# A fused SSM convolution and gated GLU on one core: the first loads of x in halves, the other two blocks behind the first weights, transposes one product earlier, ten warming matmuls

## The chip, the cores and the metric

The program runs on one core of one Trainium2 chip. The metric is the device time of the whole program in microseconds. The kernel before takes 239.67 us (median of 3 runs, 239.56 to 239.82).

## What is computed

x has 2048 rows of 640 columns in bf16. The program normalises each row, and adds to x two branches that both read the normalised rows xn: a long convolution over the sequence, gated by xn, and a gated GLU.

```python
x = A_q
xn = (x - mean(x)) / sqrt(var(x) + 1e-5)          # per row of 640
# A: short shift convolution, long FFT convolution, gate by xn
kv = (sum over t of k_pad[:, t:t+S] * shift_k[:, 3-t]) * v
y  = irfft(rfft(kv, 2S) * rfft(ssm_k, 2S))[:S] + kv * ssm_D
A  = xn * y
# B: gated GLU, 640 -> 1728 -> 640
B  = (sigmoid(xn @ w_gate) * (xn @ w_up)) @ w_down
out = x + A + B
```

## The kernel before

The 2048 rows lie as 16 blocks: partition p holds rows 16p to 16p+15, and block b is row b of each partition (128 rows of 640). Four blocks make a group; group 0 is blocks 0 to 3. The GLU works through the four groups one after another. For one group it forms 27 products of w and the transposed xn, each five matmuls of 128x128 weights by 512 columns: per 128 columns of F one gate product (`pg`) and one up product (`pu`), and one mixed product for the 64 columns left over. ScalarE takes the sigmoid of `pg` (line 266), VectorE multiplies it by `pu` into `hT` (line 272), and the down products (`pd`, line 296) follow. Between them lie the steps of the convolution (DFT by matmuls, lines 355 to 456, with round trips through DRAM). The order of all of this is a written string of letters, one per step (`ORDER`, lines 621 to 631), and every engine works through its own instructions in that order.

Ahead of the string stands a prologue, lines 469 to 508, which is where the change lies. It brings the four blocks of group 0 from x to the transposed `xnT`, and does the first two pairs of products while the blocks arrive. Five things matter in it.

- Loads. Two engines issue them: SyncE (SP) and ScalarE (ACT), each with a queue of its own that is worked in order. Lines 469 to 475 issue block 0 on SP, block 1 and then blocks 2 and 3 in one transfer on ACT, then columns 0 to 255 of w_gate on SP and of w_up on ACT, then columns 256 to 511 of both on SP. Each x block is 160 KB (128 rows of 1280 bytes), each piece of weights of 256 columns is 320 KB (640 rows of 512 bytes). The string's first letters (m) go on with the remaining loads on SP. Eight completion semaphores are shared by the loads in turn, so from the ninth load on each waits, before it is issued, for one issued earlier.
- Statistics. For each block VectorE does two `bn_stats` of 320 columns (line 198), one `bn_aggr` (202), one add (210); GpSimd takes the power (214); VectorE normalises (219). The order on VectorE is: statistics of block i, then normalising of block i-1, then aggregation of block i.
- A turn: TensorE transposes a block's five 128x128 pieces into PSUM (line 234) and ScalarE copies them to `xnT` (line 223).
- Quarters: a product of 128 instead of 512 columns, for one block (line 248), five matmuls. The first two gate and up products (`fc` 0 and 1) are made of four quarters each, block by block.
- Warming: matmuls on a zeroed tile whose result nobody reads (line 482), fifteen ahead of the first turn and two behind it.

`pt` and `idle` come from a PSUM pool with two buffers (`psC`), `pg` and `pu` from one with four (`psG`), so a fifth product waits until ScalarE has read the first.

Of the kernel before, what the change touches and what calls it, by code (L numbers as in the profile page):

```python
# [57 lines left out]
def kernel(  # L58
# [14 lines left out]
    nc = tc.nc  # L73
    xr = A_q.flatten_outer_dims().rearrange("(p b) d -> p b d", b=NB)
# [30 lines left out]
    x = res.tile([P, NB, DM], BF16, name="x")  # L105
# [15 lines left out]
    sync = nc.sync  # L121
# [49 lines left out]
    def load_w(eng, lo, hi, u):  # L171
        if u == 0:
            eng.dma_start(w[:, :, lo:hi], wgr[:, :, lo:hi])
            return
        h = min(hi, 13 * P)
        eng.dma_start(w[:, :, UP + lo:UP + h], wur[:, :, lo:h])
        if hi == FF:
            eng.dma_start(w[:, :, FF:UP], wur[:, :, h:FF])
# [51 lines left out]
    def xn_mm(g, i):  # L230
        pool, tag = (psG, "g") if g else (psC, "c")
        xts[i] = pt = pool.tile([P, NC, P], BF16, name="pt", tag=tag)
        for c in range(NC):
            nc.tensor.transpose(pt[:, c, :], xn[:, 4 * g + i, c * P:(c + 1) * P], ident[:])  # L234

    def xn_ev(g, i, copy=act_copy):
        copy(out=xnT[:, i, :, :], in_=xts[i][:, :, :])
# [4 lines left out]
    def quarter(u, fc, i):  # L242

        if i == 0:
            pgs[u, fc] = psG.tile([P, 512], F32, name=("pg", "pu")[u], tag="g")
        o = u * UP + fc * P
        for c in range(NC):
            nc.tensor.matmul(pgs[u, fc][:, i * P:(i + 1) * P], lhsT=w[:, c, o:o + P], rhs=xnT[:, i, c, :],  # L248
                             start=(c == 0), stop=(c == NC - 1))
# [216 lines left out]
        nc.vector.tensor_tensor(xs, xs, chunks[c]["yx", m][:, :, :], ALU.add)  # L466


    sync.dma_start(x[:, 0, :], xr[:, 0, :])
    nc.scalar.dma_start(x[:, 1, :], xr[:, 1, :])  # L470
    nc.scalar.dma_start(x[:, 2:4, :], xr[:, 2:4, :])
    for u in range(2):
        load_w((sync, nc.scalar)[u], 0, 256, u)
    for u in range(2):
        load_w(sync, 256, 512, u)

# [3 lines left out]
    def busy(n):  # L480
        for _ in range(n):
            nc.tensor.matmul(idle[:, :], lhsT=hT[:, 0, 0:P], rhs=hT[:, 0, :], start=True, stop=True)

    def turn(i):
        xn_mm(0, i)
        xn_ev(0, i)


    busy(15)
    for i in range(4):  # L490
        ln_stats(0, i)
        if i:
# [5 lines left out]
    turn(0)  # L498
    busy(2)
    for i in range(4):  # L500
        for fc in range(2):
            for u in range(2):
                quarter(u, fc, i)
            if (i, fc) in ((0, 0), (1, 0), (1, 1)):
                turn(1 + i + fc)
    for fc in range(2):
        gate_ev(0, fc)
        up_ev(0, fc)
# [158 lines left out]
```

## Time and profile before

| | |
|---|---|
| median of 3 runs | 239.67 us (239.56 to 239.82) |
| the profiled execution's own time | 239.41 us |
| its span, first to last instruction | 237.6 us |
| TensorE busy with matmuls | 231.4 us (97%) |
| VectorE busy | 190.3 us (80%) |
| ScalarE busy | 141.2 us (59%) |
| granted TensorE clock, mean | 1.000 |
| DMA | 54.82 MB, 231 GB/s |

The span is counted from the first instruction of the program; what lies around it (239.41 less 237.6) is start and end. A row of the timeline gives the start, the time, engine and line, the operation with what it writes and reads, how many instructions are merged in it, and in brackets the idle time before it with what ended that. A row of stretches gives each engine's busy time in a stretch of the span, the granted clock, the share of the DMA engines and the rate. A list of waits gives who waited for what, in total, how often and at most. The clock in these rows is what the throttle granted; whether a matmul ran at half speed at the very start is read from the spacing of the matmuls instead.

### The profile page before, as it was taken

Reading aid. Unit: us, or ns where it says so; the run is one execution under the profiler, and the core shown is the slowest. Engines: PE = TensorE matmul, PEld = TensorE weight load, DVE = VectorE, ACT = ScalarE, POOL = GpSimd, SP = SyncE. Lnnn points to the kernel's source line nnn. Section 1 sums busy time; section 2 is a strip of 40 time slices with the busy share of each in tenths; the row PEclk is TensorE's granted clock in tenths of the full one; section 3 lists DMA queues with packets and bytes.
Section 4 is the critical chain, followed back from the end, with each engine's and each line's share of the span. In section 5 each row is a group of like instructions: output and inputs, shape, how many; then the busy total and the mean of one; then the engine's idle time right before and its main releaser. Section 6 shows DMA issues by size and latency. Waiting matters only on the chain.

```text
span 237.6 us, 5553 instructions
## 1 busy us (share of the span) xinstructions
PE 231.4 (97%) x2265; PEld 135.1 (57%) x2265; DVE 190.3 (80%) x350; ACT 141.2 (59%) x178; POOL 11.2 (5%) x24
## 2 busy tenths in 40 slices
PE   8799999999999999999999999999999999999994
PEld 2564445878556455667754434577664434456782
DVE  3633889999999999999999999865585695968372
ACT  2342331728559897864888887997558858764000
POOL 4210000020000000002001000000000000000000
PEclk9999999999999999999999999999999999999999
DMA  7999999889998999999444888975939795285674
GB/s 212 292 314 233 259 322 298 183 249 284 253 311 243 253 295 297 284 267 319 148 183 152 234 230 258 227 228 203 241 109 222 186 281 123 89 238 144 196 237 134
DMA packets 88975, 54.82 MB, mean 231 GB/s; under 512 B 47670, under 2 KB 83062, under 8 KB 88694
## 3 DMA queue, kind: packets, MB, share of 16 engines
q1 hardware_dynamic: 88006, 53.66, 80.8%
q10 hardware_dynamic: 944, 0.82, 1.1%
q8 instruction: 17, 0.28, 0.5%
q14 instruction: 8, 0.07, 0.1%
HBM read 36.12 MB, written 18.35 MB: 229 GB/s over the span
## 4 chain that ended last, share of the span: by engine, by line
PE 95%; DMA 3%; ACT 0%; DVE 0%; ACTq 0%; issue 0%
PE pd L296 26%; PE pg L257 23%; PE pu L257 23%; PE psb L456 4%; PE ps L357 4%; PE ps L355 4%; PE ps L388 3%; DMA w<-in_B_w_up_dram 3%; PE psa L417 2%; PE pg L278 2%; PE pt L234 2%; PE pu L248 1%; PE pg L248 1%; ACT xnT L223 0%; DVE x L301 0%; ACT L119 0%
## 5 line engine op out<-in xcount | busy, mean ns | idle before, releaser
L257 PEld LDWEIGHTS <-w 128*128 128x128 bf16 x500 | 46.5, 98 | 54.3 <-issue 5.3
L296 PE MATMUL pd<-wd,hT 128*128 128x320 bf16 x448 | 64.3, 299 | 0.0
L257 PE MATMUL pg<-xnT,w 128*128 128x512 bf16 x250 | 62.2, 379 | 0.0
L257 PE MATMUL pu<-xnT,w 128*128 128x512 bf16 x250 | 62.1, 379 | 0.0
L296 PEld LDWEIGHTS <-hT 128*128 128x128 bf16 x448 | 42.8, 98 | 17.8 <-issue 1.7
L266 ACT ACTIVATE sig<-pg 128x512 bf16<-128x512 f32 x52 | 31.3, 605 | 30.1 <-PE pg L257 28.2
L272 DVE TENSOR_TENSOR hT<-sig,pu 128x512 bf16<-128x512 bf16 x52 | 35.2, 679 | 14.7 <-PE pu L257 9.3
L223 ACT CAST t<-ps 128x1024 bf16<-128x1024 f32 x40 | 39.1, 1023 | 11.4 <-DMA d<-t 6.3
L223 ACT CAST xz<-ps 128x1024 bf16<-128x1024 f32 x40 | 38.6, 1018 | 10.6 <-PE ps L388 10.5
L301 DVE TENSOR_TENSOR x<-pd,x 128x320 bf16<-128x320 f32 x32 | 15.4, 480 | 15.8 <-PE pd L296 15.7
L403 DVE TENSOR_TENSOR xz<-xz 128x2048 bf16<-128x2048 bf16 x20 | 24.4, 1220 | 0.2
L357 PE MATMUL ps<-kvh,S1t 128*128 128x128 bf16 x160 | 21.2, 219 | 0.0
L335 DVE TENSOR_TENSOR acc<-acc,tmp 128x1024 bf16<-128x1024 bf16 x30 | 20.7, 689 | 0.7
L355 PE MATMUL ps<-kvh,S1t 128*128 128x128 bf16 x160 | 21.2, 217 | 0.0
L333 DVE TENSOR_TENSOR tmp<-kx,sc 128x1024 bf16<-128x1024 bf16 x30 | 20.6, 687 | 0.4
L223 ACT CAST ao<-psa 128x1024 bf16<-128x1024 f32 x16 | 15.6, 1014 | 5.6 <-PE psa L417 3.5
L461 DVE TENSOR_TENSOR yx<-psb,xn 128x512 bf16<-128x512 f32 x20 | 13.8, 691 | 3.9 <-PE psb L456 2.9
L355 PEld LDWEIGHTS <-S1t 128*128 128x128 bf16 x160 | 15.5, 97 | 2.3
L357 PEld LDWEIGHTS <-S1t 128*128 128x128 bf16 x160 | 15.3, 96 | 2.3
L223 ACT COPY xnT<-pt 128x640 bf16<-128x640 bf16 x16 | 10.2, 709 | 10.8 <-PE pt L234 10.5
L198 DVE BATCH_NORM_STATS2 st<-x 128x6 f32<-128x320 bf16 x32 | 13.7, 471 | 2.8 <-DMA x<-in_A_q_dram 2.8
L401 DVE STREAM_SHUFFLE xz<-xz 128x512 f32<-128x512 f32 x20 | 14.6, 728 | 0.0
(44 smaller groups left out, 146.1 us busy)
## 6 DMA issues: line engine op xcount, KB each, us to landing
d<-t SPq DMA_DIRECT2D x20, 512.0 KB, 3.7
t<-d SPq DMA_DIRECT2D x20, 512.0 KB, 4.9
bi<-d SPq DMA_DIRECT2D x8, 512.0 KB, 5.5
d<-ao SPq DMA_DIRECT2D x6, 512.0 KB, 4.1
kx<-in_A_k_dram SPq DMA_DIRECT2D x10, 256.0 KB, 5.0
hn<-in_A_ssm_k_dram SPq DMA_DIRECT2D x20, 128.0 KB, 6.0
kvh<-in_A_v_dram SPq DMA_DIRECT2D x10, 256.0 KB, 5.2
x<-in_A_q_dram SPq DMA_DIRECT2D x3, 640.0 KB
```

Source lines behind the costliest of these rows:

```text
L223: nc.scalar.copy(out=out, in_=in_)
L257: nc.tensor.matmul(pg[:, :], lhsT=w[:, c, u * UP + fc * P:u * UP + (fc + 1) * P], rhs=xnT[:, :, c, :], start=(c == 0), stop=(c == NC - 1))
L266: nc.scalar.activation(sig[fc][:, :], pgs[0, fc][:, :], ACT.Sigmoid)
L272: nc.vector.tensor_tensor(hT[:, fc, :], sig[fc][:, :], pgs[1, fc][:, :], ALU.mult)
L296: nc.tensor.matmul(pd[:, :], lhsT=hT[:, fc, bb * P:(bb + 1) * P], rhs=wd[:, fc, 320 * half:320 * half + 320], start=(fc == 0), stop=(fc == ...
L301: nc.vector.tensor_tensor(x[:, 4 * t + bb, es], pds[bb, half][:, :], x[:, 4 * t + bb, es], ALU.add)
L333: nc.vector.tensor_tensor(d["tmp"][:, :, :], kx[:, lo + 3 - m:hi + 3 - m, :], sb(m), ALU.mult)
L335: nc.vector.tensor_tensor(d["acc"][:, :, :], d["acc"][:, :, :], d["tmp"][:, :, :], ALU.add)
L355: nc.tensor.matmul(ps[:, i, 0:P], lhsT=S1[:, b, h, :], rhs=cin[c]["kvh"][:, 0, b, :], start=True, stop=True)
L357: nc.tensor.matmul(ps[:, i, P:2 * P], lhsT=S1[:, b, h, :], rhs=hp[:, b // 2, b % 2, :], start=True, stop=True)
L401: nc.vector.stream_shuffle(z[:, 2, :, :].bitcast(F32), z[:, 1, :, :].bitcast(F32), swap)
L403: nc.vector.tensor_tensor(z[:, 1:3, :, :], z[:, 0:1, :, :].to_broadcast((P, 2, 8, P)), z[:, 1:3, :, :], ALU.mult)
```

## The change

Six things change, all in the prologue. Blocks 0 and 1 of x are loaded in column halves, one half on SP and the other on ACT, block 0 first. The first weights (columns 0 to 255) come next, ahead of blocks 2 and 3. Blocks 2 and 3 follow as one transfer each, block 2 on SP and block 3 on ACT. Then SP goes on as before. There are ten warming matmuls ahead of the first turn instead of fifteen. The turn of block i+1 is issued behind the first quarter of block i; before, turn 1 came behind the first two quarters of block 0, turn 2 behind the first two of block 1, and turn 3 behind the last of block 1. For block 0 the two gate quarters now come ahead of the two up quarters.

```diff
-    sync.dma_start(x[:, 0, :], xr[:, 0, :])
-    nc.scalar.dma_start(x[:, 1, :], xr[:, 1, :])
-    nc.scalar.dma_start(x[:, 2:4, :], xr[:, 2:4, :])
-    for u in range(2):
-        load_w((sync, nc.scalar)[u], 0, 256, u)
+    for b in range(2):
+        for i in range(2):
+            (sync, nc.scalar)[i].dma_start(x[:, b, 320 * i:320 * i + 320], xr[:, b, 320 * i:320 * i + 320])
+    for i in range(2):
+        load_w((sync, nc.scalar)[i], 0, 256, i)
+    for i in range(2):
+        (sync, nc.scalar)[i].dma_start(x[:, 2 + i, :], xr[:, 2 + i, :])
     for u in range(2):
         load_w(sync, 256, 512, u)
...
-    busy(15)
+    busy(10)
...
     turn(0)
     busy(2)
     for i in range(4):
-        for fc in range(2):
-            for u in range(2):
-                quarter(u, fc, i)
-            if (i, fc) in ((0, 0), (1, 0), (1, 1)):
-                turn(1 + i + fc)
+        for k in range(4):
+            fc, u = divmod(k, 2) if i else (k % 2, k // 2)
+            quarter(u, fc, i)
+            if k == 0 and i < 3:
+                turn(i + 1)
```

## The prediction

> **What bounds the kernel now.** I read the page's busy times first, then TensorE's waits, then the timeline of the first 15 us. TensorE's waits, all of them:
>
> ```profile
> PE idle L482 <- DVE hT L117: 1.2, 1, 1.2
> PE pu L248 <- DMA w<-in_B_w_up_dram: 0.6, 1, 0.6
> PE pt L234 <- DVE xn L219: 0.6, 1, 0.6
> PE pg L248 <- ACT xnT L223: 0.6, 2, 0.3
> ```
>
> All four lie in the prologue. The stretch from the first full product to the last matmul has no gap (220.02 us busy of 220.06):
>
> ```profile
> 14.34:234.40 220.06, 220.02 (x2151) 1.00 0.82 231
> ```
>
> So the end is the start of the first full product, 14.34, plus 223.26 us that the change does not touch: 237.6 in all, and 1.81 us around the span give 239.41 in the profiled execution (the median of the runs is 0.26 above it). The question is when line 257 starts. The timeline of the prologue:
>
> ```profile
> 3.97 0.89 DVE L198 BATCH_NORM_STATS2 st<-x 128x6 f32<-128x320 bf16 x2 [2.85 <-DMA x<-in_A_q_dram]
> ...
> 6.71 0.88 DVE L198 BATCH_NORM_STATS2 st<-x 128x6 f32<-128x320 bf16 x2
> ...
> 7.50 0.43 DVE L219 TENSOR_SCALAR xn<-x,mv,rstd 128x640 bf16<-128x640 bf16 x1
> ...
> 8.81 0.45 PE L248 MATMUL pu<-xnT,w 128*128 128x128 bf16 x5 [0.60 <-DMA w<-in_B_w_up_dram]
> ...
> 9.10 0.44 PE L234 MATMUL pt<-ident,xn 128*128 128x128 bf16 x5
> ...
> 10.32 0.44 PE L248 MATMUL pg<-xnT,w 128*128 128x128 bf16 x5 [0.22 <-ACT xnT L223]
> ...
> 10.35 0.45 DVE L219 TENSOR_SCALAR xn<-x,mv,rstd 128x640 bf16<-128x640 bf16 x1 [0.66 <-POOL rstd L214]
> ...
> 14.34 1.24 PE L257 MATMUL pg<-xnT,w 128*128 128x512 bf16 x5
> ```
>
> Block 0 arrives at 3.95. VectorE then works without a gap until 9.7; a block takes it 1.45 us (statistics at 5.21, 6.71, 8.16). TensorE stands from 8.2 to 8.81 for w_up, which ACT issued at 1.65 behind 480 KB of x; the chain of waits names it too (1.65 7.12 DMA w<-in_B_w_up_dram). From 8.81 TensorE is nearly full: fifteen quarters and three turns of 0.28 us each (spacing 0.056 us) are 5.0 of the 5.53 us to 14.34.
>
> How fast the loads move, by stretches of 1 us (last column GB/s):
>
> ```profile
> 2.00:3.00 1.00, 1.00 (x4) 0.44 (x3) 0.00 (x0) 0.65 (x2) 1.00 (x3) 1.00 0.77 212
> 3.00:4.00 1.00, 1.00 (x4) 0.32 (x3) 0.03 (x1) 0.00 (x0) 0.04 (x1) 1.00 1.11 367
> 4.00:5.00 1.00, 1.00 (x6) 0.44 (x5) 0.97 (x3) 0.00 (x0) 0.00 (x0) 1.00 1.05 372
> 5.00:6.00 1.00, 0.97 (x5) 0.24 (x3) 0.96 (x4) 0.00 (x0) 0.56 (x1) 1.00 1.13 303
> ```
>
> The DMA engines are full from 3 us on, so an order of loads decides who comes early; nothing comes early for free.
>
> **The change, part by part.**
>
> *Fewer warming matmuls.* Before, fifteen run from 1.18 to 5.97: by their weight loads seven at a spacing of 0.43 (1.58, 2.01 to 3.72), from 4.08 on seven in 1.39, 0.2 each. The tenth of these ends at 4.9. The first turn waits for xn of block 0 (6.54 before, later than both), so they cost and save nothing on the path. What covers this is the clock staying up (a rival below).
>
> *Loads.* Ahead of the first weights stand 328 kB (x0, x1) in place of 655 kB, so w_gate and w_up of columns 0 to 255 have moved when 983 kB have. By the rates above (0.02 MB before 2 us, then 0.21, 0.37, 0.37) that is 5.0 us, and with the lag from last packet to landing 5.8 to 6.1. The lag is about 0.7: the ACT queue's packets of w_up end near 8.05 and it lands at 8.77. The wait at 8.81 is gone; the first quarter, at 7.5, finds both weights. What is late next is block 2. SP now issues two halves, w_gate, then block 2, its fourth DMA (issues there take 0.39 to 0.53 us, so about 2.1; block 2 left ACT at 1.22 before), and in the rings 983 kB stand ahead of blocks 2 and 3. All 1311 kB have moved at 6.1 by the same rates (1.27 MB by 6.0, then 293 GB/s). To that come 0.15 for the 512 packets of 640 bytes (an estimate: between half of a 1280-byte packet's time, no loss, and the whole, 0.9 us), 0.7 of lag and 0.15 because the engines do not finish together: block 2 lands at 7.1. Bounds: 6.4, if ACT's queue falls behind SP's as it did before, and 7.9, if the small packets cost like whole ones.
>
> *What is queued behind block 2.* VectorE's statistics of block 2 wait for it, and in its order the normalising of block 1 stands behind them, though its rstd is long there. Before, these statistics ran at 6.71; with block 0 landing a little sooner (two queues share its 160 KB; I take 3.7, bounds 3.4 and 4.1) VectorE could begin them at 6.45. They start at 7.1.
>
> *Turns.* From those statistics on, by rows: xn of block 1 ends 1.22 later (6.71 to 7.93), turn 1 begins 0.06 after that, its quarter 1.22 after the turn (9.10 to 10.32: transposes, ScalarE's copy of 0.69, two hand-overs), the next turn one quarter (0.28) later. That is 1.50 per turn in the new order; VectorE's xn comes every 1.43 and is ahead (xn2 2.67, xn3 4.09 after the statistics, turns 2 and 3 at 2.78 and 4.28). TensorE has five groups of 0.28 in each 1.50, so it is not the limit either. Block 3's first quarter comes 1.50+1.50+1.22 = 4.22 after turn 1, and the first full product four quarters later (1.12; ScalarE's first sigmoid frees its buffer just then, as before). The sum from the statistics of block 2: 1.22+0.06+4.22+1.12 = 6.62.
>
> *The sum.* 7.1+6.6 = 13.7 against 14.34: 0.6 us sooner. The later weights do not bind: the order behind 1311 kB is unchanged, columns 512 to 767 of w_gate are issued around 2.8 before and are used four products after 14.34. After 14.34 everything moves up with TensorE, except loads that the DMA rate fixes. The nearest is the first half of k: VectorE's first kv step is at 23.85, its load was issued at 15.28 with 7.6 us to landing (about 22.9), so about 1 us of slack, enough for 0.6. Profiled 239.41 - 0.6 = 238.8; on the median 239.67 - 0.6 = 239.1.
>
> *A rule that speaks against the split.* The Trainium skill's DMA: Bandwidth & Descriptors (Issuing engines are not separate DMA queues) says that DMAs from different engines end up on the same 16 DMA engines and interleave, so that spreading them saves only issue time. By it the halves bring block 0 no sooner than 3.95; the forecast of 239.1 stays, since block 2 binds, but the best case below would end at 238.7 instead of 238.3. The trace agrees so far as the rate stays near 290 to 370 GB/s with one queue or two.
>
> **Rivals.**
>
> 1. *Block 2 early; VectorE is the limit.* w_up was issued with the second w_gate piece (1.65 and 1.64), yet landed at 8.77 against 7.9: between 5 and 6 us ACT's queue moved 108 packets and SP's 496. If ACT again begins its weights late, w_gate has the engines to itself and block 2 lands by 6.4. Then VectorE's own chain counts: block 0 at 3.4 to 3.7, statistics of block 2 at 2.74 later, 6.62 more: 12.8 to 13.1, so 238.1 to 238.5. Against it: both weights are now issued alike. Chance 0.13.
> 2. *Hidden anyway.* Block 2 at 7.4 to 7.9, or a later load that takes the gain back: first product 14.0 to 14.5, 239.3 to 239.9. For it: DMA share 1.0 and more up to 25 us. Chance 0.15.
> 3. *Slower by the clock.* Between the tenth warming matmul (4.9) and turn 1 (8.4) TensorE has only turn 0, two warming matmuls and one quarter, 1.0 us of work in 3.4. If the clock drops, 128-column matmuls take twice 0.056, the five groups of a turn's period 2.7 in place of 1.5, and 2 to 3.4 us at half speed cost 0.8 to 1.4 us: 239.9 to 240.5. It decides against the change once more than 0.6 us is lost. Against it: from 232.7 to 236.1 TensorE was busy 1.66 of 3.4 and in 6 to 9 us 1.51 of 3.0, at full clock. Chance 0.13.
>
> The Trainium skill's TensorE: Matmul & The Clock Gate (What's actually happening) puts the gate on free-running windows of about 3.4 us, one busy to open, one idle to close. By it ten matmuls at 0.43 are 4.3 us, enough to open, and no gap here is a whole window, so 239.1 would stand. The trace opened after 2.9 us; how busy a window must be no run here shows.
>
> 4. *Block 3 late.* It is ACT's fourth DMA and waits, by the eight semaphores, for a half of block 0 (about 3.8, plus 0.4 to issue), behind SP's later weights. From its landing to the first product are 2.64 (8.16 to 10.80) + 0.06 + 1.22 + 1.12 = 5.04, so it decides from 9.3 on; at 9.8 the time is 240.2. Against it: only w_up stands ahead in its own queue. Chance 0.07.
>
> **Numbers.** The forecast (block 2 between 6.5 and 7.4, 238.4 to 239.4) has 0.52. A measurement tells about 0.2%, 0.48 us, from no change, so below 239.19 is faster and above 240.15 slower. Faster: 0.33 of the forecast's 0.52 (block 2 before 7.2) and rival 1, 0.46. Slower: 0.09 of rival 3, 0.05 of rival 4 and 0.03 of rival 2, whose later loads may cost more than the gain, 0.17. The same: the rest, 0.37. The range leaves out the lower part of rival 1 (0.05) and most of what is slower (0.14): 238.3 to 240.2.
>
> **What would show it.** No wait of `pu` for w_up; VectorE's second long wait ended by DMA of x ahead of the statistics of block 2, at about 7.1; turns 1.5 apart; line 257 first at 13.7; matmuls without a gap after it. Wrong if spacing in the quarters is 0.11 (clock), if block 3 is what VectorE waits for, or if new waits on DMA appear after 14 us.

## The result, and the profile after

The changed kernel takes 243.57 us (median of 4 runs, 242.03 to 244.18) beside 239.75 us for the kernel before (4 runs, 239.56 to 241.14): a ratio of 1.0141 [1.0107, 1.0176], so 1.4% slower. The forecast was 239.1, with a range from 238.3 to 240.2. The profiled execution took 243.84 us with a span of 242.1, against 239.41 and 237.6 before: 4.5 us more span.

TensorE's waits in the profile after (who waits for what; total, times, longest):

```profile
PE pt L234 <- DVE xn L219: 1.8, 2, 1.3
PE pg L248 <- DMA w<-in_B_w_gate_dram: 1.4, 1, 1.4
PE idle L484 <- DVE hT L117: 1.2, 1, 1.2
PE psa L417 <- ACT t L223: 0.8, 2, 0.5
```

The wait for w_up is gone, as forecast. In its place stand a wait for w_gate, one for a normalised block, and one far from the edit: `psa` (line 417) near 127 us. The timeline after shows how the prologue ran (start, time, engine and line, operation, and in brackets the idle time before it with what ended that):

```profile
3.00 0.89 DVE L198 BATCH_NORM_STATS2 st<-x 128x6 f32<-128x320 bf16 x2 [1.88 <-DMA x<-in_A_q_dram]
...
5.57 0.45 PE L234 MATMUL pt<-ident,xn 128*128 128x128 bf16 x5 [0.49 <-DVE xn L219]
...
7.82 0.71 PE L248 MATMUL pg<-xnT,w 128*128 128x128 bf16 x5 [1.36 <-DMA w<-in_B_w_gate_dram]
...
8.59 0.89 DVE L198 BATCH_NORM_STATS2 st<-x 128x6 f32<-128x320 bf16 x2 [2.77 <-DMA x<-in_A_q_dram]
...
9.88 0.72 PE L234 MATMUL pt<-ident,xn 128*128 128x128 bf16 x5 [1.35 <-DVE xn L219]
...
10.92 1.27 PE L248 MATMUL pu<-xnT,w 128*128 128x128 bf16 x10
...
12.52 0.74 PE L234 MATMUL pt<-ident,xn 128*128 128x128 bf16 x5
...
14.93 0.44 PE L234 MATMUL pt<-ident,xn 128*128 128x128 bf16 x5
...
17.28 1.02 PE L257 MATMUL pg<-xnT,w 128*128 128x512 bf16 x4
```

Block 0's first half is there at 3.0 (the second at 3.16; before, 3.95), and turn 0 starts at 5.57 (6.54 before). Then everything waits: w_gate lands at 7.77, block 2 at 8.56. The two turns that follow are 2.64 and 2.41 apart instead of the 1.50 forecast, and a group of five 128-column matmuls shows 0.74 instead of 0.44. The first full product starts at 17.28, 2.94 us later than before.

The loads move more slowly for a while. The stretch from 3 to 4 us after, which had 367 GB/s before (from and to, length; then busy time and count of PE, PEld, DVE, ACT and POOL; then granted clock, DMA share, GB/s):

```profile
3.00:4.00 1.00, 1.00 (x4) 0.32 (x3) 0.96 (x3) 0.00 (x0) 0.04 (x1) 1.00 0.76 158
```

And the clock falls. The same kind of rows, cut at the times where the trace shows the granted clock change (4.40, 7.81, 14.64):

```profile
0.99:4.40 3.41, 3.22 (x8) 1.19 (x9) 1.46 (x6) 1.49 (x2) 2.00 (x5) 1.00 0.67 164
4.40:7.81 3.41, 1.57 (x10) 0.49 (x8) 1.39 (x5) 0.69 (x1) 1.13 (x2) 1.00 1.10 325
7.81:11.22 3.41, 2.06 (x18) 1.80 (x19) 2.60 (x9) 0.59 (x1) 0.55 (x1) 0.50 1.13 286
11.22:14.64 3.42, 3.42 (x35) 3.42 (x33) 0.76 (x4) 0.80 (x2) 1.19 (x2) 0.50 0.99 272
```

After a stretch of 3.41 us in which TensorE was busy 1.57 (46%), the clock (the first column behind the counts) is 0.50 for two such stretches, 6.83 us.

From 17.28 on TensorE keeps a constant distance of 2.94 us to the kernel before, up to the wait at `psa`. The chain of waits after, and below it the timeline, in the order of time:

```profile
121.50 4.78 DMA d<-t
```

```profile
121.50 7.15 SPq L369 DMA_DIRECT2D d<-t  x3
...
126.38 1.93 ACT L223 CAST t<-ps 128x1024 bf16<-128x1024 f32 x2 [1.68 <-DMA d<-t]
...
127.45 0.39 PE L417 MATMUL psa<-xz,SMt 32*32 32x512 bf16 x2 [0.31 <-ACT t L223]
...
128.36 0.65 PE L417 MATMUL psa<-xz,SMt 32*32 32x512 bf16 x30 [0.53 <-ACT t L223]
```

The same place before:

```profile
118.50 5.68 SPq L369 DMA_DIRECT2D d<-t  x3
...
121.91 1.93 ACT L223 CAST t<-ps 128x1024 bf16<-128x1024 f32 x2 [0.21 <-DMA d<-t]
...
124.06 0.65 PE L417 MATMUL psa<-xz,SMt 32*32 32x512 bf16 x32
```

A write of `t` to DRAM (line 369, 512 KB) took 4.78 us; before it took 3.31 (issued at 118.50). ScalarE waited 1.68 for it in place of 0.21, and TensorE stood behind ScalarE. From there on the distance is 4.28 us, and it stays so to the end. So TensorE lost 1.35 here by the starts of its matmuls. (The list of waits has 0.8 of it: the 0.39 shown for the first two `psa` matmuls hold a part of the standstill, as before all 32 took 0.65.) So 4.28 of the 4.5 us have two places: 2.94 in the prologue and 1.35 at the write.

### The profile page after: what moved, and what is told of

Its sections match the earlier page's. It is cut to its first block, busy times and chain, and to the rows that moved or that the text cites. A ratio compares the mean times of both kernels' runs of the same rounds, so it can differ in the third digit from the quotient of the medians.

```text
span 242.1 us, 5546 instructions
## 1 busy us (share of the span) xinstructions
PE 233.4 (96%) x2260; PEld 137.1 (57%) x2260; DVE 190.8 (79%) x350; ACT 141.1 (58%) x178; POOL 11.2 (5%) x24
## 4 chain that ended last, share of the span: by engine, by line
PE 90%; DMA 5%; ACT 2%; issue 1%; DVE 1%; SPq 1%; ACTq 0%
PE pd L296 24%; PE pu L257 22%; PE pg L257 22%; PE psb L456 4%; PE ps L357 3%; PE ps L355 3%; PE ps L388 3%; DMA x<-in_A_q_dram 3%; PE psa L417 2%; PE pt L234 2%; DMA d<-t 2%; PE pg L278 2%; PE pu L248 1%; ACT t L223 1%; PE pg L248 1%
## 5 line engine op out<-in xcount | busy, mean ns | idle before, releaser
L257 PEld LDWEIGHTS <-w 128*128 128x128 bf16 x500 | 46.5, 98 | 54.3 <-issue 5.3
L198 DVE BATCH_NORM_STATS2 st<-x 128x6 f32<-128x320 bf16 x32 | 13.7, 472 | 4.6 <-DMA x<-in_A_q_dram 4.6
```

The lines of the kernel that those rows point to most:

```text
L257: nc.tensor.matmul(pg[:, :], lhsT=w[:, c, u * UP + fc * P:u * UP + (fc + 1) * P], rhs=xnT[:, :, c, :], start=(c == 0), stop=(c == NC - 1))
```

## The experiments

Three causes had to be told apart: the late loads, the clock, and the slow write. Each run has the kernel before beside it on the same chip (medians 239.47 to 239.8); the ratio is to that, with its 95% interval. Warming matmuls that an experiment adds write the tile that nobody reads. "First full product" is the start of line 257, 14.34 before and 17.28 after.

### The clock: e1 and e2

e1_after_warm15 is the changed kernel with fifteen warming matmuls again, e2_before_warm10 the kernel before with ten.

```diff
e1, against the changed kernel
-    busy(10)
+    busy(15)
e2, against the kernel before
-    busy(15)
+    busy(10)
```

> The changed kernel with fifteen warming matmuls instead of ten. Theory A, the ten matmuls let the clock fall: with fifteen the granted clock stays 1.00, block 2 still lands near 8.6, the first full product starts 6.65 later, near 15.2 instead of 17.28, and the time is 240.3 to 240.7. Theory B, the late loads let it fall whatever the warming: the quarters still run at a spacing of 0.107 in part, mean clock 0.986 to 0.993, 242 to 244.

> The kernel before with ten warming matmuls instead of fifteen, nothing else. Theory A: the clock falls here too (from 4.0 to 7.4 us TensorE would be busy some 1.4 of 3.4, against 1.3 in the changed kernel), the first full product moves from 14.34 to 15.3 or later, 240.6 to 242. Theory B: clock 1.00, 239.6 to 239.8, no change.

e1: 240.19 us (10 runs), ratio 1.0024 [1.0006, 1.0041]. Its loads were as late as in the changed kernel (w_gate 7.72, block 2 at 8.58), its clock stayed at 1.0, and its first full product is at 15.24. So with the same landings the clock is worth 17.28 - 15.24 = 2.04 us, and what remains of the 2.94 is 0.90 from the late loads. The slow write is gone too (sixteenth completion 3.19 us behind the issue, no wait at `psa`). By the starts of TensorE's matmuls near the end, e1 is 3.39 ahead of the changed kernel, which is 2.04 + 1.35. That the medians differ by the same 3.38 (243.57 - 240.19) is in part luck: the two profiled executions are 3.03 apart (243.84 and 240.81), and the runs of one kernel differ in clock and landings.

e2: 240.98 us (9 runs), 1.0057 [1.0021, 1.0093]. Ten matmuls instead of fifteen, with no load moved in the program, made the kernel slower. TensorE's waits in the profile of e2, and the stretch ahead of its fall of the clock (8.60 to 15.43 at 0.50; first full product at 17.39):

```profile
PE pu L248 <- DMA w<-in_B_w_up_dram: 1.7, 1, 1.7
...
PE psa L417 <- ACT t L223: 0.5, 1, 0.5
```

```profile
5.19:8.60 3.41, 1.61 (x14) 0.75 (x12) 3.34 (x12) 0.69 (x1) 1.61 (x3) 1.00 1.16 295
```

This one profile overstates the price: in it w_up landed at 9.52 instead of 8.77, its last completion 0.84 behind the one before, so the half-speed stretches had a longer wait in them (1.7 instead of 0.6). The stretch that ended at 8.60 was over before w_up landed in either kernel. Two of its nine runs show a mean clock of 0.993 or less (242.72, 243.5); the others, at full clock, still take 240.16 to 241.22. So the fewer matmuls cost something that is not the clock: the wait at `psa` is there too.

The changed kernel once more, on another chip (f1_after_again, no edit):

> The changed kernel unchanged, more runs beside the others. By the theory of three terms (late landings 0.9, clock closing in a part of the runs about 2, instruction fetch into the d<-t write 1.35): runs at a full clock (1.0) at 239.7 + 1.35 = 241.0 to 241.7, runs whose clock was granted at 0.993 or 0.986 at 242.5 to 244.2; median between 241 and 244. By the rival that the clock loss belongs to every run of this kernel: all runs at 0.986 to 0.993 and the median within 243.2 to 243.8. Here the weights and blocks landed late in every profile with halves but one, so some runs may come in 0.9 lower.

241.55 us (5 runs, 240.5 to 241.99), 1.0063 [1.0035, 1.0092]. Two runs at 0.993, three at full clock (241.61, 240.74, 240.5). The rival that the clock falls in every run is out. In the profiled execution the clock fell for one stretch: from 5.41 to 8.83 TensorE was busy 1.52 of 3.42, then came 3.41 us at 0.50. The loads were 1.1 us less late (w_gate 6.68, block 2 at 7.50), and the first full product is at 15.60. The size of the loss thus depends on where the 3.41 us stretches lie and on how late the loads are, and both change from run to run. The 243.57 and 241.55 are one kernel.

Over all profiles with a record of the clock (all but f2), a change came only at steps of 3.41 us, and whether the clock was kept for the next stretch went with TensorE's busy time in the one that ended:

| stretch of 3.41 us at full clock | TensorE busy | next clock |
|---|---|---|
| f3, 7.68 to 11.10 (below) | 15% | 0.5 |
| f1, 5.41 to 8.83 | 44% | 0.5 |
| after, 4.40 to 7.81 | 46% | 0.5 |
| e2, 5.19 to 8.60 | 47% | 0.5 |
| e1, 8.00 to 11.41 | 51% | 1.0 |
| e8, 7.70 to 11.11 (below) | 52% | 1.0 |
| f6, 3.84 to 7.25 (below) | 54% | 1.0 |
| e7, 4.09 to 7.50 (below) | 56% | 1.0 |

All other stretches up to 14 us were 59% busy or more and kept it. The ends of the kernels narrow the boundary. By the same steps of 3.41 us, the last stretches with matmuls in the kernel before and in e7 were 49% and 48% busy and kept the clock:

```profile
232.70:236.11 3.41, 1.66 (x13) 0.98 (x10) 0.78 (x2) 0.00 (x0) 0.00 (x0) 1.00 0.56 192
```

```profile
232.78:236.19 3.41, 1.63 (x13) 0.95 (x10) 0.75 (x2) 0.00 (x0) 0.00 (x0) 1.00 0.59 199
```

The clock there stays at 1.0 until 239.53 and 239.61, a further stretch without any matmul. So the boundary lies between 47% (e2) and 48% (e7) by these busy times, which is finer than they can be trusted to be, since the ends of matmuls are modelled. At half clock, stretches 60% (after) and 72% (e2) busy did not bring it back; full ones did.

### The slow write: e7, e8, f6 and g1

The trace has packets of 16 KB on queue 8, of kind instruction: 17 in every kernel but e3, which has twelve more matmuls and as many more weight loads, and 18 packets. One of them lies near the write: at 118.8 before, ahead of the write's first packet, and at 122.5 after, in the midst of it. The view of transfers after, from 121.4 to 126.4:

```profile
## 3 DMA queue, kind: packets, MB, share of 16 engines
q1 hardware_dynamic: 283, 1.03, 51.6%
q8 instruction: 1, 0.02, 2.1%
```

If these packets bring TensorE's instructions, ten fewer of them (five matmuls, five weight loads) move the packet later against the work. e7 is e2 with five matmuls of only 32 columns put back behind turn 0, so the count of instructions is that of before; e8 is the changed kernel with the same five (`cols` is the number of columns of a warming matmul).

```diff
e7 against e2, e8 against the changed kernel
-    def busy(n):
+    def busy(n, cols=512):
...
     busy(2)
+    busy(5, 32)
```

> The kernel before with ten warming matmuls and, behind the two of turn 0, five matmuls of 32 columns on the same tile: as many instructions on TensorE as before, so that its instruction fetches of 16 KB (256 instructions) fall where they fell. Theory C, the ten fewer instructions move a fetch into the write to DRAM that ScalarE waits for at 122 us: that wait goes, TensorE has no gap at 124, runs with a full clock take 239.3 to 239.9 and the median falls from 240.98 to 239.5 to 240.0. If C is wrong and it is the ten matmuls' effect on the clock alone: a median near 241.0 again.

> The changed kernel with the same five matmuls of 32 columns behind turn 0: instruction count restored, warming still ten. Theory C: no gap at 124, 242.0 to 242.6 where the clock falls for two windows (243.57 less 1.35). If the wait at 124 comes from the later start of the products instead: it stays, 243 to 244.

e7: 239.51 us (10 runs), 1.0015 [0.999, 1.004], in place of e2's 240.98. Its runs at full clock take 239.12 to 239.69, 1.0 to 1.5 us less than e2's; three runs at 0.993 take 241.04 to 241.81. No wait at `psa`. e8: 240.06 (10 runs), 1.0014 [0.9988, 1.0041], two of them at 0.993 (241.35, 241.8); no wait at `psa` either, first full product at 14.86. Its median is below the 242.0 to 242.6 expected, because the clock stayed up in eight of the ten runs; so the medians of e8 and the changed kernel differ by the clock too. At full clock e8 takes 239.06 to 240.43, and f1, without the five small matmuls and on another chip, 240.5 to 241.61.

The same pair without halves and without late loads: f6 is e6 (below: whole blocks, the weights ahead of blocks 2 and 3) with ten warming matmuls, g1 is f6 with the five small ones.

```diff
f6, against e6
-    busy(15)
+    busy(10)
g1, against f6
     busy(2)
+    busy(5, 32)
```

> The changed kernel with blocks 0 and 1 whole, one on each queue, and with its ten warming matmuls: only the halves are undone. By the three terms: block 2 near 6.7 and the first full product at 13.4 to 13.8 where the clock stays up (238.6 to 238.9), plus 1.0 to 1.4 at the d<-t write near 124 us for ten fewer instructions of TensorE, so 239.8 to 240.3 in runs at full clock; where the clock closes behind the warming, about 2 more (241.5 to 242.5), in 0 to 4 of 10 runs. If the loss near 124 us belonged to the late start alone, it would be gone here: 238.6 to 239.0. If the clock closes in every run with ten matmuls: 241 and more in all.

> Whole blocks, weights ahead of blocks 2 and 3, new order of turns, ten warming matmuls (239.84), and five 32-column matmuls behind turn 0, so that TensorE has as many instructions as in the kernel before. By the theory of the instruction fetch: no wait at the d<-t write near 124 us, first full product at 13.3 to 13.7, 238.4 to 238.9. If the lost microsecond belonged to the early start of the first product (a load that the DMA rate fixes): the wait near 124 us stays and the time is 239.5 to 240.0.

f6: 239.84 us (10 runs), 0.9993 [0.9963, 1.0024]; its first full product is the earliest of all, 13.30, and 0.97 of it is lost at `psa`. Its waits:

```profile
PE pt L234 <- DVE xn L219: 1.4, 1, 1.4
...
PE psa L417 <- ACT t L223: 0.5, 1, 0.5
```

g1: 239.07 (12 runs), 0.998 [0.996, 0.9999]; first full product at 13.46, no wait at `psa`, 0.17 lost there, and about 0.3 on the way to it. The time is above the 238.4 to 238.9 that was expected, and the gain over f6 is 0.8 by the medians, 0.3 by the ratios, whose intervals overlap; here the profiles carry the verdict more than the times.

All eighteen profiles, times counted from the issue of that write. Its first packet is at 0.82 in all. The trace shows sixteen completions for it, which I read as one for each DMA engine. Fifteen have come by 2.56 to 2.64 in all; the sixteenth varies:

| kernels | instruction packet starts | sixteenth completion |
|---|---|---|
| e3 (twelve more matmuls) | -1.55 | 2.60 |
| 13 with TensorE's instructions as before (before, e1, e4 to e8, f2 to f5, g1, g2) | -0.01 to 0.75 | 3.01 to 3.77 |
| f1 (ten fewer) | 0.94 | 4.30 |
| after (ten fewer) | 0.98 | 4.78 |
| f6 (ten fewer) | 1.18 | 4.53 |
| e2 (ten fewer) | 2.18 | 4.42 |

A packet well ahead of the write delays nothing; one that starts after the write's first goes with a last completion 1.7 to 2.2 us behind the other fifteen, in four of four profiles; in e7, e8 and g1, where the packet comes earlier, that late completion is gone. A late start does not explain the group: f6 is early where the others are late. That a packet inside a write delays it does not hold for every write. In the one profile of f2 (below) a packet started at 51.3, inside a write issued at 46.86; fifteen completions had come by 51.60, the last at 53.73, and TensorE lost 1.5 us. But the load issued just ahead of that write was already 0.7 late on its last completion, at 50.96, and in e4, e6, f4 and f6 a packet inside the same write (49.9 to 50.7) left its last completion only 0.01 to 0.15 behind. So f2's loss is not shown to be the packet's.

### The late loads: e3, e6, f4, f5, f3, e5

e3 is e1 with more matmuls between turn 0 and turn 1, to hold the clock up whatever the landings.

```diff
e3, against e1
-    busy(2)
+    busy(8)
...
+                if i == 0:
+                    busy(6)
                 turn(i + 1)
```

> The changed kernel's loads and turns with the clock held up: fifteen warming matmuls, eight instead of two behind turn 0, six more ahead of turn 1, all in time in which TensorE waited. The clock should be 1.00 by both theories. If the loads cost by themselves, the first full product is at block 2's landing plus 6.65, 15.0 to 15.3, and the time is 240.3 to 240.7. If the clock was all of the loss, it is 238.8 to 239.4, as forecast.

240.72 us (9 runs), 1.0039 [1.0024, 1.0054]; clock kept, first full product at 15.59. This is a miss of its design: here block 2 landed at 7.13, but the added matmuls held turn 1 up to 10.25. So the matmuls put in the path cost more here than they guard, and landings vary with the same loads.

e6 undoes the halves alone: block 0 whole on SP, block 1 whole on ACT, the rest of the new order of loads and turns kept, fifteen warming matmuls. g2 is e6 again.

```diff
e6, against e1
-    for b in range(2):
-        for i in range(2):
-            (sync, nc.scalar)[i].dma_start(x[:, b, 320 * i:320 * i + 320], xr[:, b, 320 * i:320 * i + 320])
+    for b in range(2):
+        (sync, nc.scalar)[b].dma_start(x[:, b, :], xr[:, b, :])
```

> The changed kernel with fifteen warming matmuls and blocks 0 and 1 whole, one per queue, instead of in halves; the weights still ahead of blocks 2 and 3. If it is the weights' place that makes block 2 late: block 2 lands at 7.1 to 8.6, first full product 13.8 to 15.2, 239.3 to 240.4, no better than with halves (240.19). If the halves made it late: block 2 by 7.1, 239.0 to 239.2.

> The kernel with whole blocks and fifteen warming matmuls once more, for a comparison on the same chip: 238.6 to 239.1, first full product 13.3 to 13.8, by how late the clock opens.

e6: 238.85 us (9 runs), 0.9969 [0.9957, 0.9981]; g2: 239.06 (12 runs), 0.9971 [0.9954, 0.9989]. It beats both kernels. Stretch and timeline of e6:

```profile
3.00:4.00 1.00, 1.00 (x4) 0.32 (x3) 0.33 (x1) 0.00 (x0) 0.04 (x1) 1.00 1.11 346
```

```profile
6.72 0.89 DVE L198 BATCH_NORM_STATS2 st<-x 128x6 f32<-128x320 bf16 x2 [0.23 <-DMA x<-in_A_q_dram]
...
13.74 1.24 PE L257 MATMUL pg<-xnT,w 128*128 128x512 bf16 x5
```

w_gate lands at 5.31, w_up at 6.37, block 2 at 6.70. So the weights ahead of blocks 2 and 3 are no harm; the halves are. And 346 GB/s are back.

What in the halves? f4 keeps the 640-byte packets but puts both halves of a block on the block's own queue; f5 keeps 1280-byte packets and splits by partitions over both queues.

```diff
f4, against e6
-    for b in range(2):
-        (sync, nc.scalar)[b].dma_start(x[:, b, :], xr[:, b, :])
+    for i in range(2):
+        for b in range(2):
+            (sync, nc.scalar)[b].dma_start(x[:, b, 320 * i:320 * i + 320], xr[:, b, 320 * i:320 * i + 320])
f5, against e6
-    for b in range(2):
-        (sync, nc.scalar)[b].dma_start(x[:, b, :], xr[:, b, :])
+    for b in range(2):
+        for i in range(2):
+            (sync, nc.scalar)[i].dma_start(x[64 * i:64 * i + 64, b, :], xr[64 * i:64 * i + 64, b, :])
```

> The kernel with whole blocks ahead of the weights (238.85) with one edit: both blocks in halves again, but both halves of a block on the block's own queue. So the 640-byte packets are back and the split of a block over two queues is not. If the small packets are what starves the engines: rate in 3 to 4 us 150 to 210 GB/s, block 2 lands at 8.0 to 8.6 with its last engine a microsecond behind the others, first full product 14.9 to 15.3, 239.9 to 240.4. If the split of one block over two queues is what does it: rate 330 to 370, block 2 at 6.7 to 7.1, first product at 13.7, 238.7 to 239.1. Blocks 0 and 1 land no sooner than 3.6 by either.

> The changed kernel with fifteen warming matmuls and its halves cut by partitions instead of columns: rows 0 to 63 of a block on one queue, 64 to 127 on the other, so that six transfers stand in the same order on the same queues but packets are 1280 bytes, as with whole blocks. If the packets of 640 bytes slow the loads: 330 to 370 GB/s in 3 to 4 us, blocks 0 and 1 at 3.0 to 3.9, block 2 at 6.7 to 7.1 and on its last engine no later than 0.3 behind the one before, first full product near 13.7, 238.6 to 239.1. If the number of transfers, or two queues at one block, slows them: 150 to 210 GB/s in 3 to 4 us, block 2 at 7.5 to 8.6, first product at 14.6 to 15.2, 239.8 to 240.3.

f4: 239.93 us (10 runs), 1.0 [0.9981, 1.0018]; block 2 at 7.82, first full product at 14.71. f5: 239.86 (10 runs), 1.002 [1.0, 1.004]; block 2 at 7.43, first full product at 14.10. The stretch in f4 and then in f5:

```profile
3.00:4.00 1.00, 1.00 (x4) 0.31 (x3) 0.82 (x2) 0.00 (x0) 0.04 (x1) 1.00 0.92 205
```

```profile
3.00:4.00 1.00, 1.00 (x4) 0.32 (x3) 0.50 (x2) 0.00 (x0) 0.04 (x1) 1.00 0.85 206
```

Both rates drop to about 205, so neither the split over two queues nor the small packet is needed for it; what f4 and f5 share with the changed kernel is four transfers of x in place of two ahead of the weights. f5 is no clean proof, since its issues took longer (0.54 to 0.83 us each instead of 0.4) and its weights were issued 0.3 to 0.6 later. What f5 lacks is the engine that falls behind: its last two completions of block 2 are 0.2 apart, those of f4 1.1. In the seven profiles with column halves of which w_gate comes soon after, the last completion of w_gate trails the one before it by 0.1 (e3), 0.3 (f1), 0.5 (f3), 0.9 (after) and 1.2 to 1.6 (f4, e1, e8); with whole blocks by 0.01 to 0.2. It is this last completion, more than the rate, that makes block 2 late: with column halves, and block 2 behind the weights, fifteen of its sixteen completions had come by 6.54 (e8) to 7.60 (after), with whole blocks by 6.56 (f6) to 6.89 (f2), and in e8, as early as any, the last came at 8.20. Halves are not the only way to it, as e2's w_up shows (0.84, with whole blocks). How the engines share the transfers can't be read from these traces, so the mechanism behind both stays open.

f3 puts the halves alone into the kernel before.

```diff
f3, against the kernel before
-    sync.dma_start(x[:, 0, :], xr[:, 0, :])
-    nc.scalar.dma_start(x[:, 1, :], xr[:, 1, :])
+    for b in range(2):
+        for i in range(2):
+            (sync, nc.scalar)[i].dma_start(x[:, b, 320 * i:320 * i + 320], xr[:, b, 320 * i:320 * i + 320])
```

> The kernel before with one edit: blocks 0 and 1 of x in column halves, one half on each queue; blocks 2 and 3 still go together ahead of the weights. Theory H (the halves starve the DMA engines for a while and leave one engine behind): in the stretch from 3 to 4 us the rate falls from 367 to 150 to 210 GB/s, block 0 lands near 3.0, the transfers behind it complete on their last engine 0.8 to 2 us later than on the one before it, and w_up, which was waited for until 8.81, is later still: first full product at 14.6 to 15.6, 240.0 to 241.0. Rival W (it was the order of weights and blocks, or chance of the run): the rate in 3 to 4 us stays at 340 to 370, the landings of the weights stay within 0.3 us of before (5.99, 8.77), and the time is 239.3 to 239.8, since only w_up binds here.

242.6 us (4 runs), 1.0111 [1.008, 1.0141], worse than either theory said. 150 GB/s from 3 to 4 us; w_gate at 6.92 (before 5.99), blocks 2 and 3 at 6.32 (5.66). Its waits:

```profile
PE pu L248 <- DMA w<-in_B_w_up_dram: 3.0, 1, 3.0
```

w_up is needed at 7.6 and there at 10.56. Part of that is the experiment's own: with more transfers w_up comes ninth on the shared semaphores, and ACT issued it at 3.18 instead of 1.65, once a half of block 0 had landed. In the 3.41 us of that wait TensorE was busy 15%, and the clock fell.

e5 takes the halves, then blocks 2 and 3, then the weights, with eleven and six warming matmuls.

```diff
e5, against the changed kernel
-    for i in range(2):
-        load_w((sync, nc.scalar)[i], 0, 256, i)
     for i in range(2):
         (sync, nc.scalar)[i].dma_start(x[:, 2 + i, :], xr[:, 2 + i, :])
+    for i in range(2):
+        load_w((sync, nc.scalar)[i], 0, 256, i)
...
-    busy(10)
+    busy(11)
...
-    busy(2)
+    busy(6)
```

> Blocks 0 and 1 in halves on both queues, then blocks 2 and 3, one per queue, and the weights last; the new order of turns; eleven warming matmuls ahead of turn 0 and six behind it, seventeen as before. If VectorE's chain then decides (block 0 at 3.0, statistics of block 2 at 5.75): first full product at 12.6 to 13.7, by when the clock opens and the weights land, 238.0 to 239.0. If the weights, now last, hold the first quarters (landing 8.5 or later): 239.2 to 240.

239.94 us (12 runs), 1.0022 [1.0006, 1.0037]. Block 2 at 5.58, but w_up at 9.79: TensorE waits 1.1 for it, first full product at 14.54. With x first the weights bind.

### The order of turns, and a spread of the warming: e4 and f2

e4 is the kernel before with the new order of turns and quarters alone (the last hunk of the change's diff). f2 is e6 with its seventeen warming matmuls dealt out otherwise.

```diff
f2, against e6
-    busy(15)
+    busy(11)
...
-    busy(2)
+    busy(4)
+    busy(2, 32)
```

> The kernel before with the new order of turns and quarters alone (its loads and its fifteen warming matmuls kept). If the turns' order is a gain by itself: turn 1 at 8.06, turn 2 at 9.65, turn 3 at 11.15, first full product at 13.5 instead of 14.34, 238.8 to 238.9. If it is worth nothing (TensorE full from 8.81 on either way): 239.6 to 239.8. If it is the source of the loss: over 240.

> The kernel with whole blocks, weights ahead of blocks 2 and 3 and the new order of turns (238.85), with the seventeen warming matmuls dealt out otherwise: eleven ahead of turn 0, and behind it four and two of 32 columns, so that TensorE's instructions stay seventeen plus the rest. If what is left to gain in the prologue is the start of turn 0 (its fifteen warming matmuls ran past xn of block 0 when the clock opened late, at 6.2) then turn 0 begins 0.3 to 0.6 us sooner in such runs, first product at 13.4 to 13.7, 238.4 to 238.8. If block 2 (landing 6.7, +6.6) is the limit, the time stays 238.7 to 239.0. If seven microseconds with eleven warming matmuls are too little to keep the clock, some runs are 0.9 to 2 us longer.

e4: 239.14 us (12 runs), 0.9979 [0.9964, 0.9994]; first full product at 14.11 although its clock came up late, at 6.98. The order alone gains about 0.5 us by the medians (0.1 to 0.9 by the interval). f2: 239.04 (13 runs), 0.9969 [0.9953, 0.9986]: first full product at 13.58, no clock lost in 13 runs, the same time as e6. Where the warming ends is not what is left to gain.

## Why the prediction was wrong

The forecast sum against the profile after, whose first full product is 17.28 where 13.7 was forecast:

| step | forecast | measured | difference |
|---|---|---|---|
| block 2 lands | 7.1 (6.4 to 7.9) | 8.56 | +1.46 |
| from its statistics to the first full product, full clock | 6.62 | 6.64 (e1: 8.60 to 15.24), 6.64 (f6: 6.66 to 13.30) | 0 |
| ten warming matmuls | 0 | 17.28 - 15.24 | +2.04 |
| after 14.34 | all moves up | the write of `t` late | +1.35 |

These make 4.85; the profiled time was 243.84 against 238.8 forecast for it, 5.04; 0.2 has no row here.

**"So they cost and save nothing on the path."** This step failed, twice over. The path of the data is indeed free of these matmuls. But they held the clock, and they were ten instructions in TensorE's stream. For the first, rival 3 had the mechanism, its place and even the amount of work in the gap (1.0 us in 3.4), and was given 0.13. What it was argued down with were two rows 49% and 50% busy. The second, 6 to 9 us, is no step of the clock (the steps there, 4.01 to 7.42 and 7.42 to 10.83, were 83% and 66% busy). The first happens to be one, and its 49% kept the clock by a hair. The gap in question was, by the prediction's own count, far emptier than those rows, and in the profile after that stretch was 46% busy, just under the boundary of 47 to 48%. The price was too low as well: 0.8 to 1.4 for up to 3.4 us at half speed; it was 6.83 us at half clock and 2.04, because the first of the two stretches, waiting for loads, was again not full.

The rule that the prediction weighed, the Trainium skill's TensorE: Matmul & The Clock Gate (What's actually happening), has the period right: every change here is a multiple of 3.41 us from the last. Its condition, one idle window to close, is not what the runs show: 44 to 47% busy closed it. By that sentence 239.1 stood, and it should not have been leaned on, as the prediction said that no run showed how busy a window must be.

**"To that come 0.15 for the 512 packets of 640 bytes ... and 0.15 because the engines do not finish together."** Mis-sized. In the profile after, fifteen of block 2's sixteen completions had come by 7.60 and the last at 8.56. So 0.5 lies ahead of the fifteenth completion and 0.96 behind it, where 0.30 stood for packets and engines together. The upper bound, 7.9, took the packets at their worst and left the engines' spread at its 0.15. Where the halves were not used, the same step gave 6.70 (e6), below the 7.1.

**"w_gate and w_up ... 5.8 to 6.1".** They landed at 7.77 and 8.37, for the same reason; in e6 at 5.31 and 6.37. The wait for w_up did go, and w_gate took its place.

**Block 0 "a little sooner", 3.7 (3.4 to 4.1).** It came at 3.16, sooner than the bound. The prediction read the Trainium skill's DMA: Bandwidth & Descriptors (Issuing engines are not separate DMA queues) as saying no sooner than 3.95. That was a reading of its own: the page says that the engines are shared and that a second issuing engine saves only issue time, and nothing on which of two such transfers lands first. In the traces whole blocks 0 and 1 start together and block 0 is there at 3.60 to 3.95, as is f4's at 3.65 with both halves on one queue; with its column halves on both queues, issued ahead of block 1's, it is there at 3.10 to 3.18. The gain was of no use, because block 2 binds.

**"After 14.34 everything moves up with TensorE, except loads that the DMA rate fixes."** This failed at the write of `t`: 1.35 us, where the sum has nothing. The prediction looked for a load of data with little slack and named k; the loss came at a write, and went with the place of a packet that no line of the kernel issues.

**Right:** the chain from the statistics of block 2, 6.62. With whole blocks the first full product is at 13.3 (f6) to 13.74 against 13.7, and the time 238.85 (e6) against 239.1. (In e6 the two errors of the forecast offset each other: block 2 came 0.4 sooner than forecast, and turn 0 only at 6.90, since the clock came up late and the fifteen matmuls ran on, so its chain is 7.02.) The order of turns is a gain (e4); that the place of the weights adds to it is not clear of the noise (0.9969 [0.9957, 0.9981] in e6 beside 0.9979 [0.9964, 0.9994] in e4). Rival 4 (block 3 late) did not decide: block 3 landed at 9.64, ahead of its statistics at 10.04. The forecast holds for the change without its halves and with fifteen warming matmuls.

## What to carry to other kernels

Work that computes nothing can still carry something: before it is taken away, look at what share of each 3.4 us TensorE is busy without it, and try the removal with its instruction count kept. Splitting a first transfer to bring one piece sooner was paid for here by everything issued behind it, so look at when the last engine completes the next transfers, not only at the piece. A loss that appears far behind an edit, at a fixed place, is worth a look at the packets that are not the kernel's own.

## What the runs showed of the hardware that was not expected

- The granted clock fell after stretches of 3.41 us with TensorE busy 15 to 47%, and was kept after 48% (e7) and more. Where the stretches begin varies from run to run (the clock came up from the half speed of the start between 3.84 and 6.98 us). So with ten warming matmuls and whole blocks ahead of early weights the clock fell in 0 of 10 (f6) and 0 of 12 runs (g1); where a load is waited for behind the warming, in 2 of 9 (e2), 3 of 10 (e7) and 2 of 10 (e8), and in the changed kernel in 4 of 4 and 2 of 5. With fifteen, e1 shows a mean below 0.995 in 1 of 10 runs, the kernel before in 2 of 133, and f3, with its long wait for w_up, in 3 of 4.
- Instruction packets of 16 KB on queue 8 took 0.9 to 1.7 us each near the write of `t`. Where one started after that write's first packet, the write's last completion came 1.7 to 2.2 us behind the others, and ten instructions more or less decided it (e2 240.98, e7 239.51). At an earlier write, near 46.5, packets inside it did nothing of the kind in four profiles.
- With four small first transfers of x in place of two the rate in the stretch from 3 to 4 us is 150 to 209 GB/s instead of 345 to 377, and with 640-byte packets the last completion of w_gate or block 2 is 0.3 to 1.7 us behind the one before in most profiles.
